# A retention layer followed by a two-layer product: scores ahead of the first blocks, a v product on VectorE, PSUM sums for units 5 to 7, and product sums spread over the plain second layer

## The chip, the cores and the metric

The kernel runs on one core of a Trainium2 chip. The metric is the device time of one execution in microseconds. Before the change the median of four runs is 294.08 us (293.79 to 294.86). The engines are named as the profile names them: PE is TensorE (PEld its weight loads), DVE is VectorE, ACT is ScalarE, POOL is GpSimd, and SP issues DMAs.

## The reference

Eight batches of 576 tokens with eight heads of size 64 go through retention, which is attention with a decay in place of a softmax. The result, seen as 4608 tokens of width 512, goes through two weight matrices with a leaky ReLU between them.

```python
scale = 1.0 / np.sqrt(D_)
scores = scale * np.matmul(q, k.transpose(0, 1, 3, 2))
gamma = 1.0 - 2.0 ** (-5.0 - np.arange(H))
rel = pos[:, None] - pos[None, :]
Dmat = np.where(rel >= 0, gamma[:, None, None] ** rel[None, :, :], 0.0)
attn = np.matmul(scores * Dmat[None], v)                 # B, H, S, D
x = attn.transpose(0, 2, 1, 3).reshape(B * S, H * D)     # 4608 x 512
h = x @ w_in                                             # 512 x 2048
out = np.maximum(0.01 * h, h) @ w_out                    # 2048 x 512
```

## The kernel before

**Units and groups.** The 4608 tokens are 36 units of 128 tokens, each made of two chunks of 64. Four units are a group of 512 tokens, so there are nine groups. Retention is done unit by unit, with a running state per head that is carried from chunk to chunk; the two layers are done group by group.

**One unit of retention.** `load(u)` fetches q, k and v in float32. `cast_k` makes k float16 on ACT; `cast_q` and `cast_v` (L175, L179) multiply q and v with powers of the decay, on DVE or POOL. q and k are transposed, four 128x128 blocks each: on PE for units 0 to 7 (`transpose_pe`, L200, with a copy out of PSUM at L207, on ACT for units 0 to 3 and on DVE in `turn`), by DMA for later units. `scores(u)` is 32 small matmuls (L215 for k times q, L224 for the states). Then DVE runs the settling steps: `masks` (L233) makes the masked scores in float16, `state` (L255, L257, L260 and L261) adds to the running state and `state_cast` (L276, L273) makes it float16.

**Two forms of the output.** `outputs(u)` (L291, L302) writes the part of the unit's own chunk and the part of the carried state to different places of the PSUM tile `ot`; `own` (L355, ACT) copies the first out and `add` (L360, DVE) adds the two into xT. `outputs_acc(u)` (L321, L333) lets both parts add up in PSUM, with a `drain` of PE between its two halves, and `x_copy` (L341, ACT) alone brings the sum into xT. `finish2(u)` is the first form, `finish(u)` the second followed by `state_cast` of the second chunk on ACT.

**The first layer.** `h_mm` (L373) is four matmuls for one block of 128 columns of w_in. `h_half(g, a, fb)` does two such blocks for half a group (units 4g+2a and 4g+2a+1), `h_unit(u, fb)` four blocks for one unit, `h_block` one block for a group; each ends in a leaky ReLU on ACT (L387) from PSUM. Group 0 and the halves of group 1 are done in a mixed opening order, written out by hand. The PSUM pool `acc` has four buffers, the pools of `sc` and `ot` one each.

**The second layer.** Group 0 has it plainly in `wide` (L423), 16 parts of four matmuls. Between these parts `at` places the retention of later units: `burst(u)` is the scores of unit u, the outputs of unit u-1 and the settling. All later groups use a scheme with seven instead of eight products (`seven`, L483), which needs sums and differences of its operands: `mix_weights` once (L448) and `mix(g, n, x)` for each group (L467), both on DVE. `mixes(g, n)` is the two halves of sum n.

**Order of work.** Every engine takes its instructions in the order of the program[...]. The opening is a prologue of loads on SP and POOL (POOL's queue also carries the loads of w_in, L150, and w_out, L156), then a loop over units 0 to 3 with `keep_warm` matmuls (L551, on zeros, whose result nobody reads), then a list of calls that ends in

```python
    for n in range(16):
        wide(n // 4, n % 4)
        if n in at:
            at[n]()
    early(10)
    mixes(1, 2)
    seven(1, {0: [lambda: early(11)], 4: [lambda: early(12)]})
```

Groups 2 to 8 follow in a regular loop that the change doesn't touch.

Of the kernel before, what the change touches and what calls it, by code (L numbers as in the profile page):

```python
# [18 lines left out]
def kernel(  # L19
# [9 lines left out]
    nc = tc.nc  # L29
# [89 lines left out]
    def load(u, eng=None, after=None):  # L119
        for x in (1, 0, 2):  # L120
            t = ld_pool.tile([P, H, D], FP, name=f"t32_{x}")
            t32[u, x] = t
            c = 2 * u
            same = c % CB + 1 < CB
            e = eng[x] if isinstance(eng, dict) else eng or nc.sync
            engs = e if isinstance(e, tuple) else (e,)
            n = H // len(engs)
            for j, rows in ((0, P),) if same else ((0, CH), (1, CH)):
                b, w = (c + j) // CB, (c + j) % CB
                for i, e in enumerate(engs):  # L130
                    hs = slice(n * i, n * i + n)
                    d = e.dma_start(  # L132
                        out=t[CH * j : CH * j + rows, hs],
                        in_=(q, k, v)[x][b, hs, CH * w : CH * w + rows, :].rearrange(
                            "h t d -> t h d"
                        ),
                    )
                    if after is not None and (x in after or not isinstance(after, dict)):
                        behind(d, *(after[x] if isinstance(after, dict) else after))
                        after = None  # L140
                    last_load[u, x] = d
# [28 lines left out]
    def cast_k(u):  # L170
        qk16[u] = a_pool.tile([P, 2, H, D], F16, name="qk16")
        nc.scalar.copy(out=qk16[u][:, 1], in_=t32[u, 1])  # L172
# [4 lines left out]
    def cast_v(u, eng):  # L177
        v16[u] = a_pool.tile([P, H, D], F16, name="v16")
        eng.tensor_tensor(out=v16[u], in0=t32[u, 2], in1=decay(u, 1), op=MUL)  # L179
# [29 lines left out]
    def scores(u):  # L209
        a = sc_pool.tile([P, 2, 2, NP, CH], FP, name="sc")  # L210
        sc_tiles[u] = a
        for p in range(NP):
            for g in range(2):
                for j in range(2):
                    nc.tensor.matmul(  # L215
                        out=a[half(j), g, 0, p, :],
                        lhsT=qkT[u][half(g), 1, p, half(j)],
                        rhs=qkT[u][half(g), 0, p, half(j)],
                        start=True, stop=True, skip_group_check=True,
                    )  # L220
        for p in range(NP):
            for j in range(2):
                for g in range(2):
                    nc.tensor.matmul(  # L224
                        out=a[half(g), j, 1, p, :],
                        lhsT=qk16[u][half(j), 1, 2 * p + g, :],
                        rhs=v16[u][half(j), 2 * p + g, :],
                        start=True, stop=True, skip_group_check=True,
                    )
# [40 lines left out]
    def state_cast(u, copy, js=(0, 1)):  # L270
        js = [j for j in js if live(u, j)]
        if len(js) == 2:
            copy(out=st16[u], in_=s32s[u])  # L273
        else:
            for j in js:
                copy(out=st16[u][:, j], in_=s32s[u][:, j])  # L276
# [117 lines left out]
    def h_half(g, a, fb):  # L394
        ts = slice(a * HT, (a + 1) * HT)
        hps = acc_pool.tile([P, 2, HT], FP, name="acc")
        for n in range(2):
            h_mm(hps, n, g, 2 * fb + n, ts)
        leaky(g_tile(g)[:, 2 * fb : 2 * fb + 2, ts], hps)

    def h_unit(u, fb):
        g, t0 = u // 4, (u % 4) * P
        ts = slice(t0, t0 + P)
        hps = acc_pool.tile([P, 4, P], FP, name="acc")
        for n in range(4):
            h_mm(hps, n, g, 4 * fb + n, ts)
        leaky(g_tile(g)[:, 4 * fb : 4 * fb + 4, ts], hps)
# [32 lines left out]
    def mix_weights(n, x):  # L440
        fs = slice(x * HF // 2, (x + 1) * HF // 2)
        a, b = (
            (w_part(0, 1), w_part(0, 0)),
            (w_part(1, 1), w_mix[:, 0]),
            (w_part(1, 1), w_part(0, 1)),
            (w_part(1, 0), w_mix[:, 1]),
        )[n]
        nc.vector.tensor_tensor(out=w_mix[:, n, fs], in0=a[:, fs], in1=b[:, fs], op=SUB)  # L448
# [99 lines left out]
    def keep_warm(n):  # L548
        t = acc_pool.tile([P, 1, TOK], FP, name="acc")
        for _ in range(n):  # L550
            nc.tensor.matmul(out=t[:, 0, :], lhsT=idle[:, 0:P], rhs=idle, start=True, stop=True)  # L551
# [12 lines left out]
    load(3, {1: nc.sync, 0: nc.gpsimd, 2: nc.gpsimd}, {1: (last_load[1, 1],)})  # L564
    load_w_in(0)
    load_w_in(1)
    cast_v(3, nc.gpsimd)
    load_w_in(2)
    load(4, nc.gpsimd)
    load_w_in(3)  # L570
# [15 lines left out]
    for u in range(4):  # L586
        n = u + 1
        scores(u)
        if not u:
            keep_warm(3)  # L590
        state(u, 0)
        state_cast(u, dve_copy, (0,))
        masks(u)
        if not u:
            cast_q(1, nc.vector)
            cast_v(1, nc.vector)
        state(u, 1)
        if n < 4:
            transpose_pe(n, 1)
            transposed(n, 1, act_copy)  # L600
            if not u:
                keep_warm(3)
                outputs_acc(0)
                x_copy(0)
                keep_warm(1)
            transpose_pe(n, 0)
            transposed(n, 0, act_copy)
            keep_warm(3 if u == 1 else 2)
        if n < 3:
            cast_k(n + 1)  # L610
            cast_q(n + 1, nc.vector)
        if n < 2:
            cast_v(n + 1, nc.vector)
        state_cast(u, act_copy, (1,))
        if u == 1:
            outputs_acc(1)
            x_copy(1)
            keep_warm(2)
        elif u == 2:
            h_half(0, 0, 0)  # L620
            outputs_acc(2)
            x_copy(2)
            h_half(0, 0, 1)


    def halves(g, *items):
        for a, fb in items:
            h_half(g, a, fb)

    def cast_qv(u):  # L630
        cast_q(u, nc.vector)
        cast_v(u, nc.vector)

    def turn(u, x):
        transpose_pe(u, x)
        transposed(u, x, dve_copy)

    def settle(u):
        state(u, 0)
        state_cast(u, dve_copy, (0,))  # L640
        masks(u)
        state(u, 1)

    def finish(u):
        outputs_acc(u)
        x_copy(u)
        state_cast(u, act_copy, (1,))

    def finish2(u):
        outputs(u)  # L650
        own(u)
        add(u)

    halves(0, (0, 2), (0, 3))
    finish2(3)
    halves(0, (0, 4), (0, 5), (1, 0))
    cast_k(4)
    cast_qv(4)
    halves(0, (1, 1), (1, 2), (1, 3))
    turn(4, 1)  # L660
    halves(0, (1, 4))
    turn(4, 0)
    halves(0, (1, 5), (0, 6))
    cast_k(5)
    scores(4)
    settle(4)
    cast_qv(5)
    halves(0, (0, 7), (1, 6))
    finish2(4)
    state_cast(4, act_copy, (1,))  # L670
    turn(5, 1)
    cast_k(6)
    halves(0, (1, 7))
    turn(5, 0)
    scores(5)
    settle(5)
    cast_qv(6)
    h_unit(4, 0)
    turn(6, 1)
    cast_k(7)  # L680
    h_unit(4, 1)
    finish2(5)
    state_cast(5, act_copy, (1,))
    turn(6, 0)
    h_unit(5, 0)
    scores(6)
    settle(6)
    cast_qv(7)
    h_unit(5, 1)
    turn(7, 1)  # L690
    halves(1, (0, 4))
    finish2(6)
    state_cast(6, act_copy, (1,))
    turn(7, 0)
    halves(1, (0, 5))
    scores(7)
    settle(7)
    halves(1, (0, 6), (0, 7))
    finish(7)
    def mixes(g, *ns):  # L700
        for n in ns:
            mix(g, n, 0)
# [17 lines left out]
    def ahead(u):  # L720

        if u >= NU:
            return
        cast_k(u)
        cast_q(u, nc.gpsimd)
        cast_v(u, nc.gpsimd)
        transpose_dma(u)
# [8 lines left out]
        ahead(u + 2)  # L736


    load(8, after=(w_out_loads[2],))
    load(9)  # L740
    h_unit(6, 0)
    mix_weights(0, 0)
    mix_weights(0, 1)
    h_unit(7, 0)
    for n in range(1, 4):
        mix_weights(n, 0)
        mix_weights(n, 1)
        halves(1, (1, 2 * n))
        if n < 3:
            ahead(7 + n)  # L750
            load(9 + n)
        halves(1, (1, 2 * n + 1))

    def early(u, out=True):
        burst(u, out)
# [2 lines left out]
            load(u + 5)  # L758

    at = {  # L760
        1: lambda: (ahead(10), load(12)),
        4: lambda: (burst(8, False), ahead(11), load(13)),
        9: lambda: early(9),
        11: lambda: mixes(1, 0),
        13: lambda: mixes(1, 1),
    }
    for n in range(16):
        wide(n // 4, n % 4)
        if n in at:
            at[n]()  # L770
    early(10)
    mixes(1, 2)
    seven(1, {0: [lambda: early(11)], 4: [lambda: early(12)]})

    first = [f for i in range(4) for f in (i, i + HF)]
# [47 lines left out]
```

## Time and profile before

| what | value |
|---|---|
| median of four runs | 294.08 us |
| the profiled execution | 294.24 us |
| span of its trace | 292.5 us |
| PE busy | 281.2 us (96%) |
| DVE busy | 172.3 us (59%) |
| ACT busy | 144.2 us (49%) |
| POOL busy | 106.2 us (36%) |
| granted TensorE clock | 1.0 throughout |

The profiled execution is one of the four runs. Its own time is 1.74 us over its span, which is what lies around the traced instructions. All places in time below are microseconds from the start of the span.

### The profile page before, as it was taken

How to read it: one execution, taken by the hardware profiler on the slowest of the kernel's cores; microseconds unless marked ns; L12 is line 12 of the kernel's file. 1: busy time of each engine (PE TensorE's matmuls, PEld its weight loads, DVE VectorE, ACT ScalarE, POOL GpSimd, SP SyncE). 2: the span in 40 equal slices, each digit the busy share in tenths (PEclk: the TensorE clock that was granted, in tenths of full speed). 3: DMA queues.
4: the chain of work that ended last, by engine and by line, in shares of the span. 5: the costliest groups of instructions: out<-in, count | busy, mean ns of one | idle time of the engine just before them, and what ended most of it. 6: DMA issues, size and time to landing. Idle time of an engine off the chain costs nothing.

```text
span 292.5 us, 9414 instructions
## 1 busy us (share of the span) xinstructions
PE 281.2 (96%) x4101; PEld 191.0 (65%) x4101; DVE 172.3 (59%) x294; ACT 144.2 (49%) x254; POOL 106.2 (36%) x125
## 2 busy tenths in 40 slices
PE   8988978999999999999999999999999999999994
PEld 2567776844884488448844884488448844884583
DVE  1943579917993576367645763686368536740342
ACT  4657745832326741674167417741774177306610
POOL 8689701645441236223615342334225413000000
PEclk9999999999999999999999999999999999999999
DMA  8999999699999986977798668949996151012003
GB/s 215 277 209 231 285 196 195 140 244 198 208 251 253 261 195 156 261 172 128 140 275 198 146 147 239 189 101 192 248 192 143 41 179 38 4 51 94 0 2 143
DMA packets 132218, 50.01 MB, mean 171 GB/s; under 512 B 121776, under 2 KB 126512, under 8 KB 132176
## 3 DMA queue, kind: packets, MB, share of 16 engines
q1 hardware_dynamic: 125904, 39.73, 59.9%
q0 software_dynamic: 5984, 9.57, 15.0%
q8 instruction: 32, 0.52, 0.8%
q10 hardware_dynamic: 288, 0.11, 0.1%
q14 instruction: 10, 0.08, 0.1%
HBM read 36.81 MB, written 9.44 MB: 158 GB/s over the span
## 4 chain that ended last, share of the span: by engine, by line
PE 84%; DVE 6%; DMA 4%; POOL 3%; issue 1%; ACT 0%; DVEq 0%; POOLq 0%
PE acc L373 40%; PE acc L483 34%; PE acc L423 3%; PE sc L215 3%; POOL t L132 2%; DMA w_in<-in_moe_w_in_dram 2%; DMA t<-in_v_dram 2%; DVE mix L467 1%; PE sc L224 1%; PE ot L291 1%; PE ot L302 1%; DVE xT L360 1%; DVE s L233 1%; DVE s L257 1%; DVE qkT L207 1%
## 5 line engine op out<-in xcount | busy, mean ns | idle before, releaser
L373 PE MATMUL acc<-xT,w_in 128*128 128x512 f16 (+2 forms) x752 | 130.8, 329 | 2.8 <-DVE xT L360 1.2
L387 ACT ACTIVATE gt<-acc 128x512 f16<-128x512 f32 x144 | 85.9, 598 | 59.4 <-PE acc L373 57.5
L373 PEld LDWEIGHTS <-w_in 128*128 128x128 f16 x752 | 67.8, 98 | 55.2 <-issue 3.7
L483 PEld LDWEIGHTS <-gt 128*128 128x128 f16 x640 | 61.9, 98 | 9.1
L233 DVE TENSOR_TENSOR s<-sc,cs 128x512 f16<-128x512 f32 x36 | 24.7, 686 | 43.3 <-PE sc L224 43.3
L483 PE MATMUL acc<-w_out,gt 128*128 128x256 f16 x384 | 45.9, 273 | 0.2
L273 POOL CAST st<-s 128x512 f16<-128x512 f32 x21 | 12.8, 611 | 88.2 <-DVE s L257 57.5
L175 POOL TENSOR_TENSOR qk<-t,cs 128x512 f16<-128x512 f32 x28 | 30.3, 1083 | 21.4 <-DMA t<-in_q_dram 21.4
L355 ACT COPY own<-ot 128x512 f32<-128x512 f32 x32 | 18.8, 586 | 38.5 <-PE ot L302 31.2
L179 POOL TENSOR_TENSOR v<-t,cs 128x512 f16<-128x512 f32 x29 | 33.9, 1167 | 4.1 <-DMA t<-in_v_dram 3.6
L467 DVE TENSOR_TENSOR mix<-gt 128x1024 f16<-128x1024 f16 x16 | 14.9, 938 | 28.8 <-ACT gt L387 28.8
L483 PE MATMUL acc<-w_mix,gt 128*128 128x256 f16 x256 | 30.6, 273 | 0.0
L483 PE MATMUL acc<-w_mix,mix 128*128 128x256 f16 x256 | 29.5, 273 | 0.0
L483 PEld LDWEIGHTS <-mix 128*128 128x128 f16 x256 | 25.0, 98 | 3.1 <-DVE mix L467 0.2
L172 ACT CAST qk<-t 128x512 f16<-128x512 f32 x36 | 22.3, 620 | 9.1 <-DMA t<-in_k_dram 9.1
L360 DVE TENSOR_TENSOR xT<-ot,own 128x512 f16<-128x512 f32 x32 | 21.9, 683 | 3.0 <-ACT own L355 3.0
L257 DVE TENSOR_TENSOR s<-sc,s 128x256 f32<-128x256 f32 x40 | 16.8, 419 | 5.6 <-PE sc L224 5.1
L215 PEld LDWEIGHTS <-qkT 64*64 64x64 f16 x576 | 7.9, 107 | 12.7 <-issue 11.2
L508 DVE TENSOR_TENSOR osb<-acc,u 128x512 f32<-128x512 f32 (+1 forms) x17 | 11.1, 656 | 8.0 <-PE acc L483 8.0
L276 POOL CAST st<-s 128x256 f16<-128x256 f32 x7 | 2.8, 399 | 32.2 <-DVE s L261 18.3
L423 PE MATMUL acc<-w_out,gt 128*128 128x512 f16 x64 | 14.3, 379 | 0.0
L467 DVE TENSOR_TENSOR mix<-mix,gt 128x1024 f16<-128x1024 f16 x16 | 14.0, 879 | 0.5
(52 smaller groups left out, 236.6 us busy)
## 6 DMA issues: line engine op xcount, KB each, us to landing
out_dram<-osb SPq DMA_DIRECT2D x17, 512.0 KB, 4.2
t<-in_k_dram SPq DMA_DIRECT2D x28, 256.0 KB, 4.1
t<-in_q_dram SPq DMA_DIRECT2D x25, 256.0 KB, 4.3
t<-in_v_dram SPq DMA_DIRECT2D x25, 256.0 KB, 4.6
w_in<-in_moe_w_in_dram POOLq DMA_DIRECT2D x8, 256.0 KB, 6.4
w_out<-in_moe_w_out_dram POOLq DMA_DIRECT2D x4, 512.0 KB, 10.4
t<-in_v_dram POOLq DMA_DIRECT2D x7, 256.0 KB, 5.5
t<-in_q_dram POOLq DMA_DIRECT2D x6, 256.0 KB, 5.5
```

What stands on the lines that cost most here:

```text
L172: nc.scalar.copy(out=qk16[u][:, 1], in_=t32[u, 1])
L175: eng.tensor_tensor(out=qk16[u][:, 0], in0=t32[u, 0], in1=decay(u, 0), op=MUL)
L179: eng.tensor_tensor(out=v16[u], in0=t32[u, 2], in1=decay(u, 1), op=MUL)
L233: nc.vector.tensor_tensor(out=s16s[u], in0=sc_tiles[u][:, :, 0], in1=mask_sb.unsqueeze(1).unsqueeze(1).to_broadcast([P, 2, NP, CH]), op=MUL,)
L257: nc.vector.tensor_tensor(out=to, in0=st, in1=carry[0], op=ADD)
L355: nc.scalar.copy(out=owns[u], in_=ot_tiles[u][:, :, 0:NP].rearrange("q j c t -> q c j t"))
L360: nc.vector.tensor_tensor(out=x_of(u).rearrange("q (c g) t -> q c g t", g=2), in0=ot_tiles[u][:, :, NP : 2 * NP].rearrange("q g (c j) t -> ...
L373: nc.tensor.matmul(out=hps[:, n, :], lhsT=w_in16[:, c, f * P : (f + 1) * P], rhs=xT[g][:, c, ts], start=(c == 0), stop=(c == NP - 1),)
L387: nc.scalar.activation(out=out, in_=in_, func=mybir.ActivationFunctionType.Lrelu)
L423: nc.tensor.matmul(out=ys[tb], lhsT=g_t[0][:, f, tb * P : (tb + 1) * P], rhs=w_out16[:, f, :], start=(f == 0), stop=(f == NF - 1),)
L467: nc.vector.tensor_tensor(out=z[:, fs], in0=a[:, fs], in1=b[:, fs], op=op)
L483: nc.tensor.matmul(out=r[name][:, tb, :], lhsT=lhs[:, f, tb * P : (tb + 1) * P], rhs=rhs[:, f, :], start=fresh and n == 0, stop=f == HF - ...
```

## The change

The order of the opening is rewritten. In the loop over the first units, the product of unit 3's v is issued to DVE (it was on POOL, between two loads of w_in), the last block of `keep_warm` has three matmuls in place of two, and the first two half blocks `(0, 0)` and `(0, 1)`, which stood around the outputs of unit 2, now follow the scores and the settling of unit 3. In the list, the half blocks of group 0 are dealt out anew among the steps of units 4 and 5: the casts and transposes of a unit stand after more of them. Units 5 and 6 change from `finish2` to `finish` (unit 7 had it before). Units 6 and 7 have both `h_unit` blocks, so the half blocks (1, 2) and (1, 3) of group 1's second half go away; `finish(7)` stands after `h_unit(6, 0)`. The loads and casts of units 8 to 11 (`load`, `ahead`) keep their order. In the plain second layer the sums `mixes(1, n)` stand after parts 0, 3 and 7; they stood after parts 11 and 13 and after `early(10)`.

```diff
--- before.py
+++ after.py
@@ -564,7 +564,6 @@
     load(3, {1: nc.sync, 0: nc.gpsimd, 2: nc.gpsimd}, {1: (last_load[1, 1],)})
     load_w_in(0)
     load_w_in(1)
-    cast_v(3, nc.gpsimd)
     load_w_in(2)
     load(4, nc.gpsimd)
     load_w_in(3)
@@ -605,11 +604,10 @@
                 keep_warm(1)
             transpose_pe(n, 0)
             transposed(n, 0, act_copy)
-            keep_warm(3 if u == 1 else 2)
+            keep_warm(3 if u else 2)
         if n < 3:
             cast_k(n + 1)
             cast_q(n + 1, nc.vector)
-        if n < 2:
             cast_v(n + 1, nc.vector)
         state_cast(u, act_copy, (1,))
         if u == 1:
@@ -617,10 +615,8 @@
             x_copy(1)
             keep_warm(2)
         elif u == 2:
-            h_half(0, 0, 0)
             outputs_acc(2)
             x_copy(2)
-            h_half(0, 0, 1)
 
 
     def halves(g, *items):
@@ -651,52 +647,6 @@
         own(u)
         add(u)
 
-    halves(0, (0, 2), (0, 3))
-    finish2(3)
-    halves(0, (0, 4), (0, 5), (1, 0))
-    cast_k(4)
-    cast_qv(4)
-    halves(0, (1, 1), (1, 2), (1, 3))
-    turn(4, 1)
-    halves(0, (1, 4))
-    turn(4, 0)
-    halves(0, (1, 5), (0, 6))
-    cast_k(5)
-    scores(4)
-    settle(4)
-    cast_qv(5)
-    halves(0, (0, 7), (1, 6))
-    finish2(4)
-    state_cast(4, act_copy, (1,))
-    turn(5, 1)
-    cast_k(6)
-    halves(0, (1, 7))
-    turn(5, 0)
-    scores(5)
-    settle(5)
-    cast_qv(6)
-    h_unit(4, 0)
-    turn(6, 1)
-    cast_k(7)
-    h_unit(4, 1)
-    finish2(5)
-    state_cast(5, act_copy, (1,))
-    turn(6, 0)
-    h_unit(5, 0)
-    scores(6)
-    settle(6)
-    cast_qv(7)
-    h_unit(5, 1)
-    turn(7, 1)
-    halves(1, (0, 4))
-    finish2(6)
-    state_cast(6, act_copy, (1,))
-    turn(7, 0)
-    halves(1, (0, 5))
-    scores(7)
-    settle(7)
-    halves(1, (0, 6), (0, 7))
-    finish(7)
     def mixes(g, *ns):
         for n in ns:
             mix(g, n, 0)
@@ -736,20 +686,74 @@
         ahead(u + 2)
 
 
+    halves(0, (0, 0), (0, 1))
+    finish2(3)
+    halves(0, (0, 2), (0, 3), (1, 0))
+    cast_k(4)
+    cast_qv(4)
+    halves(0, (1, 1), (1, 2))
+    turn(4, 1)
+    halves(0, (1, 3))
+    turn(4, 0)
+    halves(0, (0, 4))
+    scores(4)
+    settle(4)
+    halves(0, (0, 5), (1, 4))
+    finish2(4)
+    state_cast(4, act_copy, (1,))
+    halves(0, (1, 5))
+    cast_k(5)
+    cast_qv(5)
+    halves(0, (0, 6), (0, 7))
+    turn(5, 1)
+    halves(0, (1, 6))
+    turn(5, 0)
+    halves(0, (1, 7))
+    scores(5)
+    settle(5)
+    cast_k(6)
+    cast_qv(6)
+    h_unit(4, 0)
+    turn(6, 1)
+    cast_k(7)
+    h_unit(4, 1)
+    finish(5)
+    turn(6, 0)
+    h_unit(5, 0)
+    scores(6)
+    settle(6)
+    cast_qv(7)
+    h_unit(5, 1)
+    turn(7, 1)
+    halves(1, (0, 4))
+    finish(6)
+    turn(7, 0)
+    halves(1, (0, 5))
+    scores(7)
+    settle(7)
+    halves(1, (0, 6), (0, 7))
     load(8, after=(w_out_loads[2],))
     load(9)
     h_unit(6, 0)
+    finish(7)
+    h_unit(6, 1)
     mix_weights(0, 0)
     mix_weights(0, 1)
     h_unit(7, 0)
-    for n in range(1, 4):
-        mix_weights(n, 0)
-        mix_weights(n, 1)
-        halves(1, (1, 2 * n))
-        if n < 3:
-            ahead(7 + n)
-            load(9 + n)
-        halves(1, (1, 2 * n + 1))
+    h_unit(7, 1)
+    mix_weights(1, 0)
+    mix_weights(1, 1)
+    halves(1, (1, 4))
+    ahead(8)
+    load(10)
+    mix_weights(2, 0)
+    mix_weights(2, 1)
+    halves(1, (1, 5), (1, 6))
+    ahead(9)
+    load(11)
+    mix_weights(3, 0)
+    mix_weights(3, 1)
+    halves(1, (1, 7))
 
     def early(u, out=True):
         burst(u, out)
@@ -758,18 +762,18 @@
             load(u + 5)
 
     at = {
+        0: lambda: mixes(1, 0),
         1: lambda: (ahead(10), load(12)),
+        3: lambda: mixes(1, 1),
         4: lambda: (burst(8, False), ahead(11), load(13)),
+        7: lambda: mixes(1, 2),
         9: lambda: early(9),
-        11: lambda: mixes(1, 0),
-        13: lambda: mixes(1, 1),
     }
     for n in range(16):
         wide(n // 4, n % 4)
         if n in at:
             at[n]()
     early(10)
-    mixes(1, 2)
     seven(1, {0: [lambda: early(11)], 4: [lambda: early(12)]})
 
     first = [f for i in range(4) for f in (i, i + HF)]
```

## The prediction

> **What bounds the kernel now.** I first read the page's engine table and then the busy times by stretch: the opening from the first layer matmul to the plain second layer, the stretch to 80 us, the rest. The columns are the stretch, its length, and busy time of PE, PEld, DVE, ACT and POOL.
>
> ```profile
> PE 281.2 (96%) x4101; PEld 191.0 (65%) x4101; DVE 172.3 (59%) x294; ACT 144.2 (49%) x254; POOL 106.2 (36%) x125
> ...
> 17.00:57.70 40.70, 36.60 (x688) 31.35 (x689) 26.93 (x49) 26.07 (x49) 22.04 (x26) 1.00 0.99 209
> 57.70:80.00 22.30, 21.88 (x338) 12.76 (x336) 14.16 (x21) 7.56 (x13) 11.22 (x11) 1.00 1.05 217
> 80.00:292.50 212.50, 208.35 (x2867) 139.78 (x2864) 121.20 (x204) 100.66 (x174) 59.55 (x69) 1.00 0.66 153
> ```
>
> PE bounds everything after 57.7: it idles 0.42 us to 80, and nearly all of the last row's 4.15 at the very end. So what moves the start of the plain second layer moves the end by as much. In the opening PE idles 4.1 us. PE's timeline names where; brackets hold the idle time and what ended it:
>
> ```profile
> 23.03 0.93 PE L373 MATMUL acc<-xT,w_in 128*128 128x256 f16 x7 [0.33 <-DMA w_in<-in_moe_w_in_dram]
> 24.44 4.65 PE L373 MATMUL acc<-xT,w_in 128*128 128x256 f16 x41 [0.49 <-issue]
> ...
> 36.94 0.32 PE L215 MATMUL sc<-qkT 64*64 64x64 f16 x16 [0.75 <-DVE qkT L207]
> ...
> 41.39 1.05 PE L373 MATMUL acc<-xT,w_in 128*128 128x128 f16 x16 [1.18 <-DVE xT L360]
> ...
> 45.68 0.40 PE L200 MATMUL acc<-ident,qk 128*128 128x128 f16 x4 [0.39 <-DVE qk L175]
> ...
> 47.54 0.32 PE L215 MATMUL sc<-qkT 64*64 64x64 f16 x16 [0.59 <-DVE qkT L207]
> ...
> 76.19 0.32 PE L291 MATMUL ot<-s,v 64*64 64x64 f16 x16 [0.42 <-DVE xT L360]
> ```
>
> Matmul ends are modelled, so I count from one start to the next, in **steps**. Two half blocks ahead of scores step 1.84 us (30.25 to 32.09), a lone one ahead of transposes 0.87; scores 0.38 (32.09 to 32.47), `outputs` 0.38 (34.32 to 34.70), four transposes 0.22, an `h_unit` 0.91 (37.31 to 38.22), `outputs_acc` 0.89 (49.77 to 50.66). Against these the four later gaps are 0.92, 1.36, 0.46 and 0.76: 3.50 together. DVE's timeline shows their cause, an unbroken row of work with the copies that PE wants near its end:
>
> ```profile
> 39.04 0.68 DVE L175 TENSOR_TENSOR qk<-t,cs 128x512 f16<-128x512 f32 x1
> 39.64 0.69 DVE L179 TENSOR_TENSOR v<-t,cs 128x512 f16<-128x512 f32 x1
> 40.24 0.42 DVE L207 COPY qkT<-acc 128x512 f16<-128x512 f16 x1
> 40.64 0.69 DVE L360 TENSOR_TENSOR xT<-ot,own 128x512 f16<-128x512 f32 x1
> ...
> 69.41 2.23 DVE L467 TENSOR_TENSOR mix<-gt 128x1024 f16<-128x1024 f16 x2
> 71.56 2.13 DVE L467 TENSOR_TENSOR mix<-mix,gt 128x1024 f16<-128x1024 f16 x2
> 73.61 0.68 DVE L233 TENSOR_TENSOR s<-sc,cs 128x512 f16<-128x512 f32 x1
> ```
>
> The last three rows are the gap at 76.19: scores end at 73.1, but `masks` waits until 73.61 behind four sums, and the rest of DVE's row with it.
>
> **What the Trainium skill says.** "TensorEngine Tiling (Array Packing)", Key Properties: changing the tiling mode drains TensorE. The trace agrees: halves ahead of the 64x64 scores step 1.84 where 2 x 0.87 is 1.74, so I add 0.10 at each such change. "SBUF — State Buffer", SBUF: two separate sides: VectorE and GpSimd share a port pair that one locks for a whole instruction. Here the same w_mix product takes 0.64 alone (49.64, 56.65) and 1.49 beside POOL's casts.
>
> **The change, part by part**, against the profiled execution's 294.24 us.
>
> *v of unit 3.* POOL loses 2.52 us of waiting and 1.45 of work ahead of w_in's third quarter, which was issued at 15.75. The four w_in issues before it land in 6.4 to 8.4 us, so the DMA engines are full (share 1.0 to 1.2 from 10 to 22), and being issued at 11.8 brings it only about 1 us. Behind it on POOL's queue stand load(4), w_in's last quarter, loads 5 to 7 and w_out: all up to 1 us earlier; SP's load(8), which waits for w_out, too. PE's wait at 23.03 goes anyway, since the first two halves move and this quarter is then wanted at 27. On DVE the product costs 0.60 (step 9.37 to 9.97) and fits a hole of 0.59 ahead of 15.50. Without that hole it would push unit 2's masks, and PE, by 0.6.
>
> *Scores ahead.* PE no longer starts halves at 17.19. Masks of unit 2 end at 16.84, so outputs_acc(2) runs 16.9 to 17.79 (the third keep_warm matmul, 0.22, ends at 16.6, under that wait), scores(3) to 18.17, the halves (0,0) and (0,1) to 20.01, outputs(3) to 20.39, (0,2) and (0,3) to 22.13. **A new wait** follows: (1,0) needs xT of unit 3. Scores to DVE took 0.52 and settling 2.17 (20.02, 20.54, 22.71), so ACT's state_cast starts at 20.48. ACT waits for it with both leaky ReLUs and own(3) queued behind: steps 0.31, 0.97, 0.62 as at 22.71 to 24.61, then the add, 0.69. xT is there at 23.07, PE goes on at 23.13, having stood 1.0. It has then done what the kernel before had done at 23.03: loss 0.10. The pause of 0.66 before 24.44 (24.44 less 23.68, the start of the seventh at steps of 0.109, less one such step) comes after seven of eight matmuls and has no releaser. It may recur (loss 0.10) or go (gain 0.56); I take half, a gain of 0.23.
>
> *Units 4 and 5.* Steps from 23.13: scores(4) at 28.02, outputs(4) at 30.24, scores(5) at 35.51. DVE's copies lead each by one half block (0.87) against 0.21 + 0.42; casts of k on ACT come a block earlier. v of unit 4 has landed by 25.4, inside its slack. No stall.
>
> *PSUM sums for 5 and 6.* PE pays 2 x (0.89 - 0.38) = 1.02. DVE loses two adds of 0.60. own and x_copy cost ACT the same 0.59. Unit 6: scores(5) end at 35.89, transposes of k to 37.02, outputs_acc(5) ends at 38.92, transposes of q at 39.14. h_unit(5,0) needs x_copy(5), 39.1 to 39.7: **stall 0.6**. scores(6) at 40.76; its settling on DVE (0.46, 0.46, 0.21, 0.68) ends masks at 43.09, before PE wants them at 43.24. Then cast_q(7), cast_v(7) and two copies end at 45.30, scores(7) at 45.35: stall 0.03. Stalls left: 0.63 of the 3.50, 2.87 saved.
>
> *Units 6 and 7.* Two h_units (1.82) in place of two halves (1.74), 0.08. finish(7) is covered by h_unit(6,1) against x_copy's 0.8; before, h_unit(6,0) covered it: nothing. It issues no DMA, so SP's load(8) and load(9), which it is moved past, don't feel it. ahead(8) now stands behind half (1,4), so ACT casts unit 8's k near 53.3 by my steps (54.03 before), SP's transposes follow it, and part 4's burst(8) comes at 60: that lead shrinks from 4.6 to about 3.3. w_mix's products on DVE start after settling(7), near 47.3, and keep their 8.3 us (49.64 to 57.9): done before the sums want DVE.
>
> *Sums spread.* mixes(1,0) and (1,1) fall on a DVE that stood 4.69 us before 62.62; (1,2), 2.15, ends before part 9's scores. The gap at 76.19 goes: 0.49 by steps (76.19 less 75.70, which is the scores' start at 75.33 and their 0.37). POOL's casts for unit 10 then meet the sums, up to 0.45 each (1.49 against 1.04), inside a lead of over 3.
>
> Sum: 0.23 + 2.87 - 1.02 - 0.08 = 2.0, plus 0.49: wide starts 2.0 early, the end comes **2.5** early. My steps add four releases of 0.1 each too tightly, so I take **2.2**: 292.0. The profiled execution is 0.16 over the median; against the median that is 291.9.
>
> **The rivals.** *Gain eaten by loads.* From 57 us unit transposes by DMA must land before scores. Landing after issue is 2.8, 4.1, 5.5 (issues 54.72, 58.30, 74.89) and 4.5 (97.60); scores of units 8, 9, 12 and 15 follow at 62.11, 66.91, 83.66 and 104.95: leads of 4.6, 4.5, 3.3, 2.9. Over 2.2 they hold, and loads come earlier too; but DMA is at 1.0 to 1.2 there. If loads set the pace, 1 to 2 us return: 293.5.
>
> *Slower: DVE still paces units 5 to 7.* Between scores(5) and scores(7) DVE keeps 7.6 us of work in 9.5 (settling 1.6 and 2.06, four products 2.4, copies 1.5), and only some of the leads are over 0.3. If ACT's queue or that row delays every copy as now, the 3.50 stay, while 1.10 of PE work is added: 0.10 + 1.10 - 0.49 = +0.7, 294.9 (294.8 against the median). It decides where PE's idle time after 23 us exceeds 2.4 (3.50 less 1.10). Against it: both adds, 1.2 us, are gone from that row, and more halves stand between a transpose and its use.
>
> *Not done as said.* If v's product lands late on DVE, 0.6 is lost of the gain: 292.6, still faster.
>
> **How the numbers follow.** As forecast 0.77, with its own range 291.1 to 293.0 (the pause either way, the releases, the late product); loads 0.14; slower 0.09. The range to hold 8 in 10 is 291.0 to 293.7, into the loads' case. No change means within 0.3%, 0.9 us, about what a measurement can tell. Faster 0.79, same 0.12, slower 0.09.
>
> **What would show it.** Right: the plain second layer starts near 55.7; PE idles near 1 before (1,0) with own(3) at 21.8, near 0.6 before h_unit(5,0), and hardly before scores(5), (6), (7); no gap near 74. Wrong: gaps of over 0.4 before those scores, waits for qkT by DMA from 59 on, or a DVE row at 15 that ends late.

## The result, and the profile after

The changed kernel is slower in these runs, by 0.4%. Its median is 295.91 us (293.52 to 297.54, 43 runs) against 294.16 us (64 runs) for the kernel before; the ratio is 1.0041, 95% interval 1.0029 to 1.0053. The forecast was 291.9 us. The ratios leave out executions more than 1.5% above the fastest of their kernel, of which three of the experiments below have one each. The profiled execution took 295.31 us with a span of 293.5, and all places below are in such a span. Half of the listed executions lie between 293.5 and 295.4 us with a granted TensorE clock of 0.997 or more; the other half lie at 295.9 us and above, nearly all with a clock of 0.991 to 0.994. The profiled one is of the first half, so the trace shows the loss without the reduced clock: 1.07 us against the trace before (295.31 and 294.24).

The busy times by stretch (length, then PE, PEld, DVE, ACT, POOL, clock, DMA share and GB/s) say where to look:

```profile
17.00:57.70 40.70, 37.96 (x709) 32.61 (x709) 27.38 (x49) 26.75 (x51) 19.55 (x22) 1.00 0.97 207
57.70:80.00 22.30, 20.31 (x325) 11.67 (x324) 13.31 (x24) 6.86 (x13) 10.39 (x12) 1.00 0.98 211
```

PE idles less in the opening than before (2.7 us against 4.1). In the next stretch, where it had idled 0.42 us, it now idles 2.0. PE's timeline puts names to both:

```profile
24.20 2.78 PE L373 MATMUL acc<-xT,w_in 128*128 128x256 f16 x24 [0.82 <-DVE xT L360]
...
40.75 1.05 PE L373 MATMUL acc<-xT,w_in 128*128 128x128 f16 x16 [0.34 <-ACT xT L341]
...
45.57 0.40 PE L200 MATMUL acc<-ident,qk 128*128 128x128 f16 x4 [0.40 <-issue]
...
56.97 4.48 PE L423 MATMUL acc<-w_out,gt 128*128 128x512 f16 x20
...
75.25 0.32 PE L291 MATMUL ot<-s,v 64*64 64x64 f16 x16 [0.17 <-DVE xT L360]
...
77.52 1.91 PE L483 MATMUL acc<-w_out,gt 128*128 128x256 f16 x16 [1.82 <-ACT k L495]
```

The first two waits are the ones that the prediction named; the third is a pause with no releaser in the profile. The row at 56.97 is the start of the plain second layer, 0.73 us earlier than before. Then the last row takes it back: PE waits 1.82 us for **k1**, ACT's copy of the first of the seven products out of PSUM, before it may add the second product onto the same tile. No wait of this kind was in the kernel before. At the first block of group 2 the changed kernel is 1.03 us behind it (88.84 against 87.81).

Two timelines explain why ACT is late. ACT's casts of k (L172) for units 8 to 13 and the copy k1 (L495), then SP's transposes (L183) and loads of k in the same stretch:

```profile
55.04 0.61 ACT L172 CAST qk<-t 128x512 f16<-128x512 f32 x1
...
56.79 0.61 ACT L172 CAST qk<-t 128x512 f16<-128x512 f32 x1
...
60.77 0.62 ACT L172 CAST qk<-t 128x512 f16<-128x512 f32 x1 [2.87 <-DMA t<-in_k_dram]
...
65.29 0.62 ACT L172 CAST qk<-t 128x512 f16<-128x512 f32 x1 [3.41 <-DMA t<-in_k_dram]
...
70.64 0.62 ACT L172 CAST qk<-t 128x512 f16<-128x512 f32 x1 [2.98 <-DMA t<-in_k_dram]
...
76.37 0.62 ACT L172 CAST qk<-t 128x512 f16<-128x512 f32 x1 [2.80 <-DMA t<-in_k_dram]
76.89 0.58 ACT L495 COPY k<-acc 128x512 f32<-128x512 f32 x1
```

```profile
55.73 1.33 SPq L183 DMA_TRANSPOSE qkT<-qk  x1
...
59.87 1.63 SPq L183 DMA_TRANSPOSE qkT<-qk  x1
61.59 0.53 SPq L132 DMA_DIRECT2D t<-in_k_dram  x1
...
64.14 2.49 SPq L183 DMA_TRANSPOSE qkT<-qk  x1
...
68.81 2.63 SPq L183 DMA_TRANSPOSE qkT<-qk  x1
71.53 1.39 SPq L132 DMA_DIRECT2D t<-in_k_dram  x2
```

Read together they are a chain over two queues. Each engine's instructions stand in the same order in both traces of the changed kernel (149 on SP, 259 on ACT), so a late one holds up those behind it. In this stretch SP waits once, for ACT's cast of unit 8 (55.04), and starts that unit's transposes at 55.73. From there to the load of unit 13 (71.53) it issues transposes and loads in turn with no pause over 0.2 us; the later casts are done before SP comes to their transposes (unit 10: cast at 60.77, transposes at 64.14). So a late start of the chain goes through to its end. There ACT waits for SP: the load of unit 11 (61.59) for the cast at 65.29, the load of unit 13 for the cast at 76.37. k1 is next in ACT's program, and could have been copied when its product ended near 74.7.

In the kernel before, the same chain began a microsecond earlier, and the last cast waited for nothing; ACT then waited for PE instead. SP's rows, then ACT's:

```profile
54.72 1.33 SPq L183 DMA_TRANSPOSE qkT<-qk  x1
...
69.94 1.39 SPq L132 DMA_DIRECT2D t<-in_k_dram  x2
```

```profile
74.26 0.62 ACT L172 CAST qk<-t 128x512 f16<-128x512 f32 x1
75.44 0.59 ACT L495 COPY k<-acc 128x512 f32<-128x512 f32 x1 [0.55 <-PE acc L483]
```

The load of unit 13 is issued 1.59 us later than before. Of this the late start is 1.01; the rest is that SP's issues in between took longer (15.80 against 15.22). Then its second half landed 4.0 us after its issue where it had landed after 2.9. Why these two were slower isn't shown.

The chain begins later because of where the change puts it. Before, the casts of unit 8 (`ahead(8)`) stood with five blocks of the first layer still to come before the plain second layer, those of unit 9 with three. In the changed list they stand with three and with one. Their order among themselves is kept; their distance to the second layer is not.

### The profile page after: what moved, and what is told of

Read it like the earlier page. It is cut to its first block, busy times and chain, and to the rows that moved or that the text cites. A ratio compares the mean times of both kernels' runs of the same rounds, so it can differ in the third digit from the quotient of the medians.

```text
span 293.5 us, 9446 instructions
## 1 busy us (share of the span) xinstructions
PE 282.0 (96%) x4118; PEld 192.3 (65%) x4118; DVE 170.3 (58%) x293; ACT 143.9 (49%) x254; POOL 103.2 (35%) x124
## 4 chain that ended last, share of the span: by engine, by line
PE 83%; DMA 4%; SPq 4%; DVE 3%; issue 2%; ACT 1%; POOL 1%; DVEq 0%; POOLq 0%
PE acc L373 41%; PE acc L483 33%; DMA t<-in_v_dram 3%; PE sc L215 3%; SPq L132 2%; SPq L183 2%; PE sc L224 1%; PE ot L291 1%; PE ot L302 1%; DMA t<-in_q_dram 1%; PE ot L321 1%; PE acc L200 1%; DVE v L179 1%; DVE s L233 1%; PE ot L333 0%
## 5 line engine op out<-in xcount | busy, mean ns | idle before, releaser
L355 ACT COPY own<-ot 128x512 f32<-128x512 f32 x30 | 17.6, 586 | 36.5 <-PE ot L302 29.1
L179 POOL TENSOR_TENSOR v<-t,cs 128x512 f16<-128x512 f32 x28 | 31.2, 1114 | 1.4 <-DMA t<-in_v_dram 1.2
L172 ACT CAST qk<-t 128x512 f16<-128x512 f32 x36 | 22.3, 620 | 18.6 <-DMA t<-in_k_dram 13.1
L467 DVE TENSOR_TENSOR mix<-gt 128x1024 f16<-128x1024 f16 x16 | 14.1, 880 | 29.0 <-ACT gt L387 29.0
L360 DVE TENSOR_TENSOR xT<-ot,own 128x512 f16<-128x512 f32 x30 | 20.5, 684 | 4.3 <-ACT own L355 4.3
L467 DVE TENSOR_TENSOR mix<-mix,gt 128x1024 f16<-128x1024 f16 x16 | 13.1, 826 | 0.5
```

The lines of the kernel that those rows point to most:

```text
L355: nc.scalar.copy(out=owns[u], in_=ot_tiles[u][:, :, 0:NP].rearrange("q j c t -> q c j t"))
L360: nc.vector.tensor_tensor(out=x_of(u).rearrange("q (c g) t -> q c g t", g=2), in0=ot_tiles[u][:, :, NP : 2 * NP].rearrange("q g (c j) t -> ...
L467: nc.vector.tensor_tensor(out=z[:, fs], in0=a[:, fs], in1=b[:, fs], op=op)
```

## The experiments

Theory A: the casts of units 8 and 9 stand too late relative to the second layer, and the chain of loads ends in ACT's wait ahead of k1. Rival B: the new opening itself costs. Rival C: the product sums early on VectorE delay POOL's casts, and so the loads. Each kernel was timed beside runs of the kernel before on the same chip; ratios are to those.

**e1_casts_early**, one part of the change undone:

```diff
     h_unit(7, 0)
+    ahead(8)
+    load(10)
     h_unit(7, 1)
...
     halves(1, (1, 4))
-    ahead(8)
-    load(10)
+    ahead(9)
+    load(11)
...
     halves(1, (1, 5), (1, 6))
-    ahead(9)
-    load(11)
```

> The changed kernel with the casts, transposes and loads of units 8 to 11 put back to where they stood relative to the plain second layer: ahead(8) and load(10) with five blocks of the first layer still to come (three in the changed kernel), ahead(9) and load(11) with three to come (one). Theory A, the supply chain of SP and ACT (transposes of unit u, then the load of u+2, then the cast of u+2) starts too late and ACT, waiting for k of unit 13, holds up the copy k1 that PE needs: the stall of 1.82 us near 77.5 goes and with it the drop of the granted clock, 292.5 to 293.3 us, ratio to before 0.994 to 0.997, clock 0.997 or more. Rival B, the new opening itself is what costs and the place of these casts doesn't matter: 295 to 296 us, as the changed kernel.

Measured: 292.65 us (292.15 to 293.29), ratio 0.9934, interval 0.9914 to 0.9955, every clock at 0.997 or more. ACT's timeline of this kernel has the cast of unit 13 and k1 in the old relation; SP's rows follow:

```profile
73.56 0.62 ACT L172 CAST qk<-t 128x512 f16<-128x512 f32 x1
74.72 0.59 ACT L495 COPY k<-acc 128x512 f32<-128x512 f32 x1 [0.55 <-PE acc L483]
```

```profile
53.98 1.33 SPq L183 DMA_TRANSPOSE qkT<-qk  x1
...
69.78 1.39 SPq L132 DMA_DIRECT2D t<-in_k_dram  x2
```

The chain starts 1.75 us earlier than in the changed kernel, and the load of unit 13 is issued earlier by the same 1.75 us.

The second layer starts at 56.99, as in the changed kernel (56.97), so all of the difference comes after it. A loss of 0.4% has become a gain of 0.7% by the place of four calls: theory A, against B.

**e2_before_casts_late**, that one part of the change alone:

```diff
         halves(1, (1, 2 * n))
-        if n < 3:
-            ahead(7 + n)
-            load(9 + n)
+        if n > 1:
+            ahead(6 + n)
+            load(8 + n)
         halves(1, (1, 2 * n + 1))
```

> The kernel before with that one place changed: ahead(8) and load(10) with three blocks of the first layer still to come, ahead(9) and load(11) with one, and nothing else of the change. Theory A: cast of k for unit 8 near 55.8, load(10) issued near 58, ACT late at k1, a PE stall of 0.5 to 2 us between 74 and 80, 294.6 to 296.5 us. Rival B: no change, 294.1 us within 0.3.

Measured: 297.46 us (295.27 to 299.65), ratio 1.0099, interval 1.0061 to 1.0137: beyond the expected range, and enough to account for more than the whole loss. PE's timeline:

```profile
79.24 1.91 PE L483 MATMUL acc<-w_out,gt 128*128 128x256 f16 x16 [2.18 <-ACT k L495]
```

Four of the six executions had a clock of 0.992 or less.

**e3_k1_ahead_of_cast** leaves the casts of units 8 to 11 where the change put them and takes k1 out of the queue behind unit 13:

```diff
-    early(10)
-    seven(1, {0: [lambda: early(11)], ...
+    burst(10)
+    seven(1, {0: [lambda: (ahead(13), load(15)), lambda: early(11)], ...
```

> The changed kernel with the casts of unit 13 and load(15) behind the copy k1 of the first of the seven products; before that they stood ahead of it on ACT. Theory A, with ACT's order as the last link: the wait for k1 (1.82 us) goes, at most a shorter one for a later copy or a later unit's transposes comes, 293.0 to 294.6 us, and the granted clock stays at 0.997 or more. If instead PE lacks the transposes themselves, the stall moves to the scores of units 11 to 13 and the time stays at 295 to 296 us. Rival B: 295 to 296 us with the stalls in the opening.

Measured: 292.87 us median (292.49 to 298.10, the highest at a clock of 0.994), ratio 0.9936, interval 0.9913 to 0.9958: at the lower edge of the range expected. The wait for k1 is gone. A shorter one for the transposes of unit 12 has come, as PE's timeline shows:

```profile
82.79 0.32 PE L215 MATMUL sc<-qkT 64*64 64x64 f16 x16 [0.72 <-DMA qkT<-qk]
```

**e12_before_late_k1_ahead** makes the same edit in e2's kernel:

> The kernel before with the late casts of units 8 to 11 (297.5 us in an earlier run, PE waiting 2.18 us for k1) and with the casts of unit 13 and load(15) behind the copy k1. If ACT's order is the link between the late loads and PE: the wait for k1 goes, 294.4 to 295.5 us, with at most a shorter wait for transposes of units 11 or 12. If PE lacks the transposes in any case: 296 us or more.

Measured: 294.79 us (293.99 to 299.05), ratio 1.0002, interval 0.9985 to 1.0019. The wait for k1 is gone here too; one of 0.42 us for the transposes of unit 12 is left. So the late loads cost PE little by themselves; what costs is ACT standing behind a load with a copy that PE needs. ACT's order is the last link, with the new opening and without it.

**e11_casts_later_still** makes the suspected cause larger: `ahead(8)` and `load(10)` with one block still to come, `ahead(9)` and `load(11)` behind the last.

> The changed kernel with the suspected cause made larger: ahead(8) and load(10) with one block of the first layer still to come (three in the changed kernel), ahead(9) and load(11) behind the last one. That is 1.7 us and 0.9 us later on ACT. Theory A: the wait of PE for k1 grows from 1.7 or 1.8 us to about 3.0 us, and a profile or several executions with the clock at half for 3.4 us behind it: 296 to 298.5 us. Rival B, the place of these casts doesn't matter and the gain of putting them back had another reason: as the changed kernel, 294.6 to 296.

Measured: 297.35 us (295.28 to 298.79), ratio 1.0083, interval 1.0056 to 1.0111. The profiled execution (298.69 us) is one with a reduced clock. PE's timeline, then two rows of the stretches of that trace (the clock is the number ahead of the DMA share):

```profile
76.62 0.32 PE L215 MATMUL sc<-qkT 64*64 64x64 f16 x16 [2.02 <-DMA qkT<-qk]
...
78.08 0.26 PE L302 MATMUL ot<-qkT,st 64*64 64x64 f16 x8 [0.82 <-POOL st L273]
79.44 3.48 PE L483 MATMUL acc<-w_out,gt 128*128 128x256 f16 x16 [1.10 <-ACT k L495]
```

```profile
70.00:80.00 10.00, 6.06 (x157) 4.04 (x156) 6.60 (x12) 3.67 (x7) 5.00 (x6) 0.96 0.95 176
80.00:84.00 4.00, 4.00 (x27) 3.03 (x25) 0.60 (x1) 0.00 (x0) 2.40 (x3) 0.66 1.13 207
```

The stall is not one wait of 3 us, as expected, but three in a row: transposes of unit 11, POOL's cast of the state, k1. In the last of them the granted clock falls to half, for 3.41 us (79.3 to 82.7 in the trace's clock record), and the 16 matmuls at 79.44 take 3.3 us to the next group where they take 1.75 at full clock. This fits the upper half of the changed kernel's executions: a mean clock of 0.994 over 293 us is 3.5 us at half speed, 1.75 us lost, about the distance between its two groups of times (medians 294.74 and 296.44). No trace of the changed kernel itself caught it.

The counts say the same, with exceptions. A clock of 0.994 or less stands in 39 of 89 executions of the kernels whose traces stall at k1 (the changed one, e2, e4 and e11). It stands in 6 of 184 of the others, 95 of these being of the kernel before. So the reduced clock mostly comes with the stall, but also without it.

**e5_after_again**, the changed kernel unaltered:

> The changed kernel itself, unaltered, beside the others on one chip. Theory A: again two groups of times, near 294.6 and near 296.4 us; the upper group has a granted clock of 0.991 to 0.994, which is about 3.4 us at half speed (0.006 x 293 x 2), and if the profiled execution is one of these, the half clock lies between 74 and 85 us, behind the stall at k1. Rival: the half clock lies in the opening, ahead of 57 us, and then it is the opening that costs.

Measured: 294.82 us median (292.46 to 296.75), ratio 1.0002, interval 0.9980 to 1.0024. On this chip only two of 14 executions had the reduced clock. The profiled one had a wait of 1.68 us for k1 and a clock of 1.0, so it doesn't place the half clock; only e11's trace does. Whether the changed kernel is slower or even depends on how many executions fall to the reduced clock.

**e4_sums_as_before** and **e10_early_sums_as_before** put the three sums back to their old places, in the changed kernel and in e1's:

```diff
     at = {
-        0: lambda: mixes(1, 0),
         1: lambda: (ahead(10), load(12)),
-        3: lambda: mixes(1, 1),
...
-        7: lambda: mixes(1, 2),
         9: lambda: early(9),
+        11: lambda: mixes(1, 0),
+        13: lambda: mixes(1, 1),
     }
...
     early(10)
+    mixes(1, 2)
```

> The changed kernel with the three product sums at their old places (after parts 11 and 13 and after the burst of unit 10). Theory A: the stall at k1 stays, as ACT is late for k of unit 13; the gap of 0.4 us ahead of the outputs of unit 10 comes back under it, so 295 to 296.5 us. Rival C, the sums at parts 0, 3 and 7 delay POOL's casts and so the loads behind them: the stall goes and the time falls to 293 to 294 us.

> The kernel with the casts of units 8 to 11 put back to their old distance, and with the product sums at their old places too. Against 292.65 us with the sums spread: 0.2 to 0.5 us more if spreading them is worth what the prediction says, no more than 0.2 if it isn't.

**e9_before_sums_spread** makes the opposite edit in the kernel before:

> The kernel before with the three product sums at parts 0, 3 and 7 of the plain second layer, and nothing else of the change. The prediction had 0.49 us for this, the gap ahead of the outputs of unit 10. If that holds: 293.6 to 293.9 us where the kernel before has 294.1 to 294.4. If only the part of that gap goes that the later traces lost (0.25 us between the scores of unit 11 and the outputs of unit 10): no difference that can be measured. If the sums early on VectorE delay POOL's casts and with them the loads: slower by up to 1 us.

Measured: e4 294.46 us (ratio 0.9993, interval 0.9968 to 1.0017), with PE still waiting for k1 as the row below shows, so not rival C; e10 293.03 us (0.9953, interval 0.9938 to 0.9968); e9 294.81 us (1.0011, interval 0.9996 to 1.0026). e4 is 0.5 us below the range expected of it. Only 3 of its 14 executions are at reduced clock, and three at full clock take 292.4 to 292.8 us, too little for a stall of 1.8; so the stall may be missing in some executions, which no trace shows.

```profile
77.29 1.91 PE L483 MATMUL acc<-w_out,gt 128*128 128x256 f16 x16 [1.82 <-ACT k L495]
```

From the start of the plain second layer to the first block of group 2 the traces have 30.11 us before and 29.85 with the sums spread (e9), 30.11 without and 29.85 with them in e1's kernel (e10, e1). So spreading the sums is worth 0.26 us, which the times can't tell from nothing.

**e6_early_without_sums** gives units 5 and 6 their separate outputs, own and add again; **e7_early_v_on_pool** gives v of unit 3 back to POOL; both in e1's kernel.

```diff
-    finish(5)
+    finish2(5)
+    state_cast(5, act_copy, (1,))
...
-    finish(6)
+    finish2(6)
+    state_cast(6, act_copy, (1,))
```

> The kernel with the casts of units 8 to 11 put back to their old distance, and units 5 and 6 with separate outputs, own and add in place of sums in PSUM. By the steps of the prediction: PE saves 1.02 us, but h_unit(5,0) waits 0.24 us longer for own and add, DVE has two adds of 0.60 more, and the copies ahead of scores(7) come 0.5 us later: within 0.5 us of the kernel with the sums, 292.2 to 293.2 us. If the sums are what the opening's gain rests on: 294 us or more. If they cost their full 1.02 us: 291.6 us.

```diff
     load_w_in(1)
+    cast_v(3, nc.gpsimd)
     load_w_in(2)
...
-            cast_v(n + 1, nc.vector)
+            if n < 2:
+                cast_v(n + 1, nc.vector)
```

> The kernel with the casts of units 8 to 11 put back to their old distance, and v of unit 3 on POOL between the loads of w_in, as in the kernel before. If its place on VectorE costs nothing, as it fits a hole of 0.6 us there, and the loads behind POOL have over a microsecond of slack: 292.7 us within 0.4. If POOL's earlier issue of the loads is worth something by itself: 293.3 us or more.

Measured on one chip: e6 293.18 us (0.9952, interval 0.9932 to 0.9972), e7 292.77 us (0.9943, interval 0.9921 to 0.9965). e7 can't be told from e1: v on VectorE costs nothing, and the earlier loads behind it bring nothing, as far as intervals of 0.2% either way can tell. In e6's trace h_unit(5,0) waits 1.18 us instead of 0.34, and two waits of 0.40 and 0.59 that the sums had removed are back:

```profile
40.24 1.05 PE L373 MATMUL acc<-xT,w_in 128*128 128x128 f16 x16 [1.18 <-DVE xT L360]
44.54 0.40 PE L200 MATMUL acc<-ident,qk 128*128 128x128 f16 x4 [0.40 <-DVE qk L175]
46.40 0.32 PE L215 MATMUL sc<-qkT 64*64 64x64 f16 x16 [0.59 <-DVE qkT L207]
```

From scores(4) to the second layer e6 takes 28.3 us; kernels with the sums take 27.8 (e1, e3, e4, e5), 27.9 (after), 28.0 (e7), 28.1 (e11) and 28.4 (e10). So the sums pay back the 1.0 us that they cost PE, and whether they bring up to half a microsecond more stays open; the times don't separate e6 from e1 either.

**e8_early_k1_rotated** has the remedies of e1 and e3 together and lets the half block (0,4) fill PE's wait for xT of unit 3:

```diff
-    halves(0, (0, 2), (0, 3), (1, 0))
+    halves(0, (0, 2), (0, 3), (0, 4))
...
-    halves(0, (1, 1), (1, 2))
+    halves(0, (1, 0), (1, 1))
     turn(4, 1)
-    halves(0, (1, 3))
+    halves(0, (1, 2))
     turn(4, 0)
-    halves(0, (0, 4))
+    halves(0, (1, 3))
```

> Both remedies of theory A together (casts of units 8 to 11 at their old distance; casts of unit 13 and load(15) behind the copy k1), and the half block (0,4) ahead of (1,0), which takes over the 0.8 us that PE waits for xT of unit 3 (the other half blocks of units 2 and 3 move back by one place each). Theory A: no PE idle time over 0.3 us ahead of (1,0) unless the third quarter of w_in is late, 291.5 to 292.4 us. If the opening's gain is lost again in the second layer whatever is done ahead: 292.7 us, as with the casts' place alone.

Measured: 292.96 us (292.48 to 293.18), ratio 0.9938, interval 0.9915 to 0.9961: above the range expected, and no better than e1. PE's timeline shows that the wait for xT went and a pause with no releaser took its place:

```profile
23.98 2.23 PE L373 MATMUL acc<-xT,w_in 128*128 128x256 f16 x19 [0.97 <-issue]
```

No kernel here is shown better than e1's. It beats the kernel before by 0.45 to 0.86%, and with it the changed kernel, which is no faster than that one.

## Why the prediction was wrong

**The step that failed** is in "Units 6 and 7": "ahead(8) now stands behind half (1,4) ... that lead shrinks from 4.6 to about 3.3". The place was seen, the cast came at 55.04 instead of 53.3 (1.3 of these 1.7 us because the second layer itself came later than forecast), and the lead became 2.8. But it was costed by one consumer only, PE's scores. Their leads did hold, as the rival "gain eaten by loads" asked: the smallest is 1.2 us, at unit 11. What was left out is that the same four calls sit on two other queues: SP's, where each load stands behind the transposes of two units before, and ACT's, where each cast waits for that load, ahead of copies that PE needs. Starting that chain a microsecond later, while PE came earlier, cost 1.82 us at k1 (in e2 2.18 us, gone in e12, where k1 stands ahead). The half of the executions at reduced clock took 1.7 us more. With the four calls put back (e1) the time is 292.65 us, within the range that was forecast. Neither rival of the prediction had that wait. The slower rival, VectorE pacing units 5 to 7, did not happen: the waits ahead of scores(5), (6) and (7) are gone, as forecast.

**Terms of the sum.** The opening was to bring 2.0 us at the start of the second layer; it brought 0.73 in the profiled execution. Over the traces with the same opening the start lies between 56.15 and 56.99 (after, e1, e3, e4, e5, e10, e11), and between 57.15 and 58.05 with the old one (before, e2, e9, e12): means of 56.7 and 57.7, a gain of 1.0.
- From scores(4) to the second layer the steps come to 27.56 us (28.02 to 55.58); the changed kernel took 27.87. So they were right to 0.3 us, and the pause of 0.40 at 45.57, which they did not have, is more than that. The wait ahead of h_unit(5,0) was 0.34 idle, forecast 0.6 by steps.
- scores(4) was forecast at 28.02; it came at 29.10. The wait for xT of unit 3 was near the forecast of 1.0 (0.82 idle, or 0.9 by steps), but outputs_acc(2) began at 17.34, not 16.9, and paused for half a microsecond at 18.21. "It may recur (loss 0.10) or go": it went from its old place and came back at another.
- The sums were put at 0.49 and are worth 0.26; the 0.17 of idle time that remain at 75.25 are unit 9's xT, as before late on VectorE.
- v of unit 3, forecast at nothing, is nothing (e7). The sums in PSUM at least pay for themselves (e6); more can't be told.

With the chain at its old distance the forecast holds in sign: e1 gains 0.45 to 0.86%, the forecast was 0.7%. That the size fits too is partly luck. The opening brought 1.0 us where 2.0 were forecast, and the sums 0.26 where 0.49 were; together that is 0.4%.

## What to carry to other kernels

When a call that casts, transposes and loads is moved, follow each of its instructions on its own queue to what stands behind it: here the damage was not at the data's consumer but at an unrelated copy that stood behind a waiting cast on ACT. Place a prefetch by its distance to the consumer's pace, not by its neighbours in the list; if the consumer comes earlier, the start of the chain has to come earlier too, above all when a queue in it has no pause that could take up a delay (SP here had none from 55.73 to 71.53). Put copies that release PSUM for TensorE ahead of casts that wait for a load, and count a stall of about 2 us on TensorE as up to nearly 4: here 1.82 at k1 and 1.7 more in the executions at reduced clock.

## What the runs showed of the hardware that was not expected

- **The clock can halve with short stalls.** A reduced clock stands in 21 of 44 executions of the changed kernel in the first set of runs, where its trace has a single gap of 1.82 us, and in 2 of 14 on another chip (1.68 us). It stands in 9 of 11 of e11, whose trace has 3.9 us of stalls in three parts between 74 and 80. The Trainium skill ("TensorE: Matmul & The Clock Gate", HAM oscillation — how this bites in real kernels) speaks of gaps over 3.4 us; here no single gap of these stalls was longer than 2.2 us. In the one trace that caught it, e11's, the half clock lasted 3.41 us. That a single gap of 1.8 us is enough is what the counts suggest; no trace shows it.
- **Pauses with no releaser follow instruction fetches.** In the traces' DMA records a 16 KB packet of the instruction queue ends at 23.07 (before), 16.74 (after), 16.57 (e4) and 22.66 (e8); PE resumes after its pause at 24.44, 18.21, 17.95 and 23.98: 1.3 to 1.5 us later each time. The pauses of 0.30 to 0.40 us near 45 in after, e1, e3, e4, e5 and e8 fit as well. Of twelve such pauses over 0.2 us between 10 and 110 us in all traces, eleven end 1.3 to 1.5 us after such a packet. But each trace has 12 or 13 such packets in that time and at most two pauses, so most packets bring none. This is a coincidence often seen, not tested. It would explain why filling one wait (e8) only uncovered another.
- **A VectorE cast and a DMA issue on POOL hold each other up.** The cast at 8.59 took 0.76 us in the changed kernel and 0.29 before, where it started at 8.56, though the program ahead of it is the same. The long one ends 0.12 us after POOL's issue of 8.34 ends; with the short one, POOL's issue took 0.99 us instead of 0.89. It comes and goes between kernels that don't differ up to there: 0.46 to 0.70 us in e1, e4, e5, e7 and e11, where the cast started at 8.66 or later, and 0.29 to 0.32 in the others, where it started by 8.56. It put the outputs of unit 0 at 10.00 instead of 9.60. The Trainium skill's "SBUF — State Buffer", SBUF: two separate sides, describes such a lock between the two engines.
